# Attention phases beside a token mixer: one inversion step a phase later, one pairing changed, nine products in the last outputs

## The chip, the cores and the metric

The kernel runs on one core of one Trainium2 chip. Its time is the device time of one execution in microseconds, given as the median of several runs. The engines are named as in the profile: PE is TensorE (matmuls; its weight loads are listed apart as PEld), DVE is VectorE, ACT is ScalarE, POOL is GpSimd and SP is SyncE, which here mainly issues DMAs. Each engine works through its own queue of instructions in order and waits at a semaphore when something it needs is not ready.

## The reference

With x of 2048 tokens by 512 channels, the result is a gated sum of two branches, `g * a + (1 - g) * b`.

```
g = sigmoid((x * gate_w).sum(-1))
a: qkv = x @ wqkv, 32 heads of 16 channels
   p = softmax(q k^T * 16**-0.5);  a = concat_heads(p v) @ wo
b: h = layernorm(x);  u = gelu(h^T @ w1 + b1)      (512 x 1792, over tokens)
   b = (u @ w2 + b2)^T                             (2048 x 512)
```

Everything is float32. The kernel keeps that precision in its large products by splitting a number into a high and a low part and adding three products (high by high, high by low, low by high).

## The kernel before, in words

The kernel first projects v, k and q, normalises the rows and runs the first layer of the mixer. This takes the first 300 us or so. The rest, from about 305 us to the end, is the attention, with the second mixer layer and the output projection packed between its instructions. The order of all instructions of this part is written out by hand, so each engine's queue is exactly the order in which the Python loop issues them.

**Groups and phases.** A group is one half of the queries (1024) with one pair of heads; there are 32 groups (16 pairs of heads for each half). A group has 4 phases, so there are 128 phases, numbered 0 to 127 (`LAST`). A phase makes 16 score tiles of 128 keys by 512 queries (n = 0 to 15). A score product uses only 64 of TensorE's 128 rows: head 0 of the pair lies in rows 0 to 63, head 1 in rows 64 to 127. Two products on different halves of the rows can run side by side.

**Dense products beside scores.** Because of that, the first `n_b` scores of a phase are all of one head (head 0 in an even phase, head 1 in an odd one), and beside each of them runs one half of a dense product (`dn`), 64 of its 128 rows. The even phase does one half of the rows, the next odd phase the other half. The remaining 16 − n_b scores alternate between the heads, so that two of them run side by side. The dense products are the second mixer layer up to phase 91 (n_b = 14), none in phases 92 to 95, the output projection of the first 8 row tiles in phases 96 to 111 (n_b = 12, all of a tile's products), and that of the last 8 row tiles in phases 112 to 127. Of those last tiles only a part is done there: 6 products (phases 112 to 117, three tiles) or 8 (phases 118 to 127, five tiles) of the 12. The remaining products, which need the last heads, are done in the tail after phase 127 (`others`, with `early[t]` the number already done). There the last pair of heads is multiplied directly (`last_pair`), and the rows are finished on VectorE and stored (`finish`, line 1039).

**From scores to v.** The 16 score tiles lie in seven PSUM banks, used in turn. Four (n = 1, 3, 5, 7) are copied out by VectorE (line 930) and go through one closing exponential on ScalarE at the end of the phase (line 945, tile `pe`). Six (n = 0, 2, 4, 6, 8, 9) take one ScalarE exponential each (line 934). The last six are taken in three pairs of neighbouring banks, (10, 11), (12, 13) and (14, 15), with one exponential for each pair (line 875), or two in a group's first phase for the first of them (line 878). A bank is free again only when the copy or the exponential that reads it is done; the scores n >= 10 wait for that.

Then `apply_v` multiplies the exponentials with v, pair of tiles by pair of tiles, in the order `TURNS` = (0, 2), (4, 6), (8, 9), (10, 11), (12, 13), (14, 15). The pairs (1, 3) and (5, 7) and the last one are held over to the next phase. In the first phase of a group the held pairs of the previous group are applied first (its final add), then the new group's pairs go to another bank. The product v accumulates in one bank, whose columns are split by head, and VectorE adds the bank to the group's sum `ot` (line 821): one instruction over 512 columns if both heads and both query blocks are met, otherwise one instruction for each part that was met (128 or 64 partitions by 256 columns).

**Sums, inversion and fetching.** v has a column of ones, so the softmax denominators come out as rows of `ot`. When a group is final, `store` writes its outputs and its row sums `r` to DRAM. For every four pairs of heads (one k of 4, for each half of the queries) `invert(half, k, pairs, at)` then brings the sums back (DMA `inv<-r`, line 623, issued in phase p0), clamps and inverts them on VectorE (lines 626 and 627, in the phase `at`, after that phase's copies and before its `ot` add), and stores them again (DMA `ri<-inv`, line 631, in phase `at + 1`). `fetch_o` loads the unnormalised outputs (line 641) and the inverted sums broadcast over 16 rows each (line 642), and lets VectorE multiply, round to the high part and subtract to the low part (line 955). For the second half and k = 2 this is p0 = 113 and `at` = 113; the fetch is called in phase p2 = 114, with its VectorE steps in phases 115, 115 and 116, and `load_wq` in p2 + 4 = 118.

`calls[p]` are issued at the start of phase p, mostly DMAs on SP and a memset on POOL; `later[p]` are VectorE steps issued after the copies of phase p. The lines that decide this:

```
        calls.setdefault(at + 1, []).insert(0, (put_back,))
    ...
            for what, *args in calls.get(p, ()):
    ...
            for what, *args in later.get(p, ()):
    ...
            turns, now_held = ([tuple(units[n] for n in pair) for pair in pairs] for pairs in (order, HELD))
```

Of the kernel before, what the change touches and what calls it, by code (L numbers as in the profile page):

```python
# [59 lines left out]
def gated_mix(ctx: ExitStack, tc: tile.TileContext, a_x, a_wqkv, a_wo, b_w1, b_b1, b_w2, b_b2, gate_w, out):  # L60
# [54 lines left out]
    order = {f0: [(c + (NS // 2 if f0 + NB >= F else 0)) % NS for c in range(NS)] for f0 in range(0, F, NB)}  # L115
# [51 lines left out]
    with tc.tile_pool(name="vp", bufs=1, side="right") as pool:  # L167
# [140 lines left out]
        y, t, w = (pool.tile([P, NS], F32, name=n) for n in "ytw")  # L308
# [34 lines left out]
    with tc.tile_pool(name="ln0", bufs=3, side="right") as ln:  # L343

        def project(w, n):
            ps = bank()
            cols = slice(n * NB, (n + 1) * NB)
            hi, lo = w
            products(ps, [((hi[:, k, :], lo[:, k, :]), (xt_hi[:, k, cols], xt_lo[:, k, cols])) for k in range(ND)])
            return ps  # L350
# [68 lines left out]
    with tc.tile_pool(name="ln1", bufs=3, side="right") as ln, tc.tile_pool(name="gl", bufs=2, side="right") as gl:  # L419
# [29 lines left out]
        for f0, cs in order.items():  # L449
            n = min(NB, F - f0) // P  # L450
# [37 lines left out]
    NP = H // 2  # L488
# [42 lines left out]
    PHASES, NSC, BANKS = 4, 16, 7  # L531
# [15 lines left out]
    def second_layer(t):  # L547

        box = []

        def step(fc, k):
            if fc == 0 and k == 0:
                box.append(ps_dn.tile([P, D], F32, name="dn"))
            if fc % 4 == 0 and k == 0:
                load_weight()
                box.append(ready.pop(0))
            at = slice(fc % 4 * P, (fc % 4 + 1) * P)
            hi, lo = (w[:, at] for w in box[-1])
            a, b = ((hi, u_hi), (hi, u_lo), (lo, u_hi))[k]
            last = fc == NF - 1 and k == 2  # L560
            return box[0], a, b[:, fc, :], fc == 0 and k == 0, last, (lambda: second_out(t, box[0])) if last else None

        return [(step, fc, k) for fc in range(NF) for k in range(3)]
# [4 lines left out]
    def call(at, *what):  # L568
        calls.setdefault(at, []).append(what)
# [140 lines left out]
    def put(steps, at, sizes):  # L710
        for n in sizes:
            dense[at] = [steps.pop(0) for _ in range(n)]
            at += 1
        assert not steps
        return at

    def put_output(t, m, at):
        steps, load = project(t, m)
        call(2 * at - 2, load)
        return put(steps, at, [m])  # L720
# [4 lines left out]
    first, at = steps[:28], put(steps[28:], 0, [14])  # L725
    for t in range(1, NS):
        at = put(second_layer(t), at, [14] * 3)
    for half in range(2):
        for k in range(ND):
            pairs = 3 if half and k == ND - 1 else 4  # L730
            p0 = PHASES * (half * NP + 4 * k + pairs) + 1
            call(p0, invert, half, k, pairs, p0 + (0 if half and k > 1 else 2))
    p0 = 2 * at
    call(p0, open_end)
    on_dve(p0 + 9, end_constants)
# [5 lines left out]
    for t in range(NH):  # L741
        at = put_output(t, 3 * ND, at)
    p1 = PHASES * (NP + 2 * 4) + 3
    call(p1, fetch_o, 1, 0, (8, 9), (p1 + 2, p1 + 3, p1 + 3))
    call(p1 + 4, fetch_o, 1, 1, (10, 11), (p1 + 6, p1 + 7, p1 + 7))
    p2 = PHASES * (NP + 3 * 4) + 2
    assert p2 > 2 * at
    call(p2, fetch_o, 1, 2, (0, 1), (p2 + 1, p2 + 1, p2 + 2))
    call(p2 + 4, load_wq, p2 + 4)
    call(LAST - 1, fetch_o, 1, 3, (2, 3), (LAST, LAST, LAST), 3)  # L750
    for t in range(NH, NS):
        at = put_output(t, 6 if 2 * at < p2 + 3 else 8, at)
    assert at == NG * PHASES // 2

    token = out_pool.tile([1, 1], F32, name="token", bufs=1)
# [4 lines left out]
    TURNS = [(0, 2), (4, 6), (8, 9), *TWO]  # L760
    HELD = [(1, 3), (5, 7)]
# [64 lines left out]
    with tc.manual_schedule(engines=engines):  # L826
# [4 lines left out]
        for n, (step, *args) in enumerate(first):  # L831
            if n and n % 12 == 0:
                split_weight(nc.vector.tensor_copy, nc.vector.tensor_tensor)
            ps, a, b, start, stop, done = step(*args)
# [4 lines left out]
        for p in range(LAST + 1):  # L839
            grp, ph = divmod(p, PHASES)  # L840
            second = ph % 2
            if ph == 0:
                sums[grp] = ot_pool.tile([P, NB], F32, name="ot")
                nc.gpsimd.memset(sums[grp], 0.0)
                at = [[0, 0], [0, 0]]
# [8 lines left out]
            n_b = len(beside)  # L854
            half = slice(0, HALF) if second else slice(HALF, P)

            head = [second if n < n_b else (n - n_b) % 2 for n in range(NSC)]
            qbs = {}
            for a, b in TURNS + HELD:
                if head[a] == head[b]:  # L860
                    qbs[a], qbs[b] = 0, 1
                else:
                    zero, one = (a, b) if head[a] == 0 else (b, a)
                    qbs[zero], qbs[one] = turn, 1 - turn
                    turn = 1 - turn

            swap = ph == PHASES - 1 and p < LAST and n_b == NSC - 2
            order = [*TURNS[:4], TURNS[5], TURNS[4]] if swap else TURNS

            def exps(n):  # L870
                pt = ptp.tile([P, 2, NB], F32, name="p2", bufs=len(TWO) + 1)
# [16 lines left out]
            for n in range(NSC):  # L888
# [31 lines left out]
                if n < n_b:  # L920
                    ps, a, b, begin, last, done = beside[n]
# [218 lines left out]
```

## Time and profile before

| what | value |
|---|---|
| median of 3 runs | 1293.45 us (1293.15 to 1293.7) |
| profiled execution | 1294.68 us |
| its span, first to last instruction | 1292.5 us |
| mean granted TensorE clock | 0.996 |
| busy: PE, ACT, DVE, POOL | 99%, 84%, 52%, 15% of the span |
| HBM traffic | 101 GB/s over the span |

A timeline row gives the start and the time in microseconds, the engine, the line of the kernel, the operation, the tiles written and read, the shapes and the count of merged instructions; in square brackets stands how long the engine had been idle before it and what ended that. SPq and ACTq are DMAs issued by those engines. Times are counted from the start of the span. A wait for several semaphores is put down to the one that came last. Matmul ends are modelled, so the distance between two starts says more than a matmul's own time.

### The profile page before, as it was taken

Reading aid. Unit: us, or ns where it says so; the run is one execution under the profiler, and the core shown is the slowest. Engines: PE = TensorE matmul, PEld = TensorE weight load, DVE = VectorE, ACT = ScalarE, POOL = GpSimd, SP = SyncE. Lnnn points to the kernel's source line nnn. Section 1 sums busy time; section 2 is a strip of 40 time slices with the busy share of each in tenths; the row PEclk is TensorE's granted clock in tenths of the full one; section 3 lists DMA queues with packets and bytes.
Section 4 is the critical chain, followed back from the end, with each engine's and each line's share of the span. In section 5 each row is a group of like instructions: output and inputs, shape, how many; then the busy total and the mean of one; then the engine's idle time right before and its main releaser. Section 6 shows DMA issues by size and latency. Waiting matters only on the chain.

```text
span 1292.5 us, 33044 instructions
## 1 busy us (share of the span) xinstructions
PE 1275.1 (99%) x13276; PEld 838.4 (65%) x13276; DVE 671.4 (52%) x1142; ACT 1088.5 (84%) x1537; POOL 198.0 (15%) x306
## 2 busy tenths in 40 slices
PE   9999999999999999999999999999999999999997
PEld 7888888886666666666666666666665556655555
DVE  5675362437445545445445444544544675545555
ACT  3443343448999999999999999999999999998993
POOL 0210244454111111111111111111110000000000
PEclk9999999999999999999999999999999999998999
DMA  4497643327343343333444433333423755433412
GB/s 131 139 317 277 223 120 98 98 78 160 67 88 76 73 96 83 79 62 82 84 69 89 82 75 60 80 81 68 86 55 87 163 125 121 89 78 88 80 37 79
DMA packets 93581, 133.19 MB, mean 103 GB/s; under 512 B 16277, under 2 KB 55339, under 8 KB 90348
## 3 DMA queue, kind: packets, MB, share of 16 engines
q1 hardware_dynamic: 92844, 129.94, 41.4%
q8 instruction: 107, 1.75, 0.6%
q10 hardware_dynamic: 576, 1.05, 0.2%
q14 instruction: 54, 0.44, 0.1%
HBM read 97.00 MB, written 33.93 MB: 101 GB/s over the span
## 4 chain that ended last, share of the span: by engine, by line
PE 88%; ACT 9%; issue 1%; DVE 1%; SPq 0%; DMA 0%; ACTq 0%
PE av L799 27%; PE s L913 20%; PE acc L417 12%; PE t L913 11%; PE acc L74 10%; PE s L799 4%; ACT p L934 3%; ACT p L875 3%; ACT pe L945 2%; PE dn L922 2%; PE pa L996 1%; PE acc L188 1%; PE dn L835 1%; PE acc L255 0%; DMA inv<-r 0%
## 5 line engine op out<-in xcount | busy, mean ns | idle before, releaser
L934 ACT ACTIVATE p<-s 128x512 f32<-128x512 f32 x768 | 413.2, 783 | 8.1 <-PE s L913 7.8
L875 ACT ACTIVATE p<-t 128x1024 f32<-128x1024 f32 x352 | 365.6, 1264 | 0.0
L913 PE MATMUL s<-qs,ks 64*128 64x512 f32 x1344 | 339.1, 403 | 4.2 <-DVE ot L821 3.6
L930 DVE COPY pe<-s 128x512 f32<-128x512 f32 x512 | 317.8, 682 | 5.6 <-PE s L913 4.9
L913 PEld LDWEIGHTS s<-qs,ks 64*128 64x128 f32 x1344 | 231.9, 184 | 104.1 <-issue 51.9
L799 PE MATMUL av<-p,v 128*32 128x256 f32 x4904 | 289.5, 380 | 0.0
L821 DVE TENSOR_TENSOR ot<-av,ot 128x512 f32<-128x512 f32 (+2 forms) x137 | 83.3, 609 | 393.0 <-PE av L799 392.8
L945 ACT ACTIVATE pe<-pe 128x2048 f32<-128x2048 f32 x129 | 276.8, 2148 | 0.0
L799 PEld LDWEIGHTS av<-p,v 128*32 128x32 f32 x4904 | 159.8, 110 | 106.6 <-issue 2.0
L913 PE MATMUL t<-qs,ks 64*128 64x512 f32 x704 | 180.2, 451 | 4.5 <-DVE pe L930 0.3
L922 PE MATMUL dn<-u_hi,w_lo 64*128 64x512 f32 x430 | 174.8, 406 | 0.0
L922 PE MATMUL dn<-u_lo,w_hi 64*128 64x512 f32 x430 | 174.7, 406 | 0.0
L922 PE MATMUL dn<-u_hi,w_hi 64*128 64x512 f32 x428 | 173.5, 405 | 0.0
L67 POOL TENSOR_TENSOR w_lo<-w_raw,w_hi 128x512 fp32r<-128x512 f32 (+1 forms) x126 | 149.0, 1189 | 124.5 <-ACT w_hi L66 108.0
L913 PEld LDWEIGHTS t<-qs,ks 64*128 64x128 f32 x704 | 89.5, 185 | 91.5 <-ACT p L934 89.9
L926 POOL MEMSET token<- 1x1 f32 x124 | 11.2, 91 | 830.9 <-PE dn L922 739.9
L799 PE MATMUL av<-pe,v 128*32 128x256 f32 x2048 | 138.1, 387 | 0.0
L66 ACT CAST w_hi<-w_raw 128x512 fp32r<-128x512 f32 (+1 forms) x67 | 38.1, 569 | 79.2 <-PE acc L417 58.8
L799 PEld LDWEIGHTS av<-pe,v 128*32 128x32 f32 x2048 | 53.6, 109 | 55.2 <-ACT p L934 31.3
L417 PE MATMUL acc<-h_hi,w_hi 128*128 128x512 f32 x224 | 87.1, 389 | 0.0
L417 PE MATMUL acc<-h_lo,w_hi 128*128 128x512 f32 x224 | 87.1, 389 | 0.0
L417 PE MATMUL acc<-h_hi,w_lo 128*128 128x512 f32 x224 | 87.1, 389 | 0.0
(150 smaller groups left out, 1513.3 us busy)
## 6 DMA issues: line engine op xcount, KB each, us to landing
w_raw<-in_B_w_dram SPq DMA_DIRECT2D x96, 256.0 KB
ks<-kp SPq DMA_DIRECT2D x192, 128.0 KB
qs<-qp SPq DMA_DIRECT2D x256, 64.0 KB
qp<-pc SPq DMA_DIRECT2D x16, 768.0 KB
x<-in_A_x_dram SPq DMA_DIRECT2D x32, 256.0 KB
kp<-pc SPq DMA_DIRECT2D x16, 512.0 KB
w_raw<-in_B_w_dram SPq DMA_DIRECT2D x32, 128.0 KB
bp<-row SPq DMA_DIRECT2D x16, 256.0 KB
```

What stands on the lines that cost most here:

```text
L66: copy(hi, src)
L67: return sub(lo, src, hi.bitcast(F32), ALU.subtract)
L74: nc.tensor.matmul(ps, a, b, start=start and n == 0, stop=stop and n == last)
L417: nc.tensor.matmul(p, a, b, start=first and k == 0, stop=last and k == 2)
L799: mm = nc.tensor.matmul(av[32 * j : 32 * (j + 1), i * QC : (i + 1) * QC], v_flat[:, v_at : v_at + 32], pt[:, h * QC : (h + 1) * QC], start ...
L821: nc.vector.tensor_tensor(x, y, x, ALU.add)
L875: nc.scalar.activation(pt, twos[low, low + 1], AF.Exp, scale=SCALE)
L913: nc.tensor.matmul(s, kt[grp][rows_i, c * P : (c + 1) * P], qt[grp][rows_i, qb * NB : (qb + 1) * NB], start=True, stop=True,)
L922: mm = nc.tensor.matmul(ps, a[half], b[half], start=begin and not second, stop=last and bool(second))
L930: nc.vector.tensor_copy(pt, s)
L934: nc.scalar.activation(pt, s, AF.Exp, scale=SCALE)
L945: nc.scalar.activation(x, x, AF.Exp, scale=SCALE)
```

## The change

There are three edits. The first gives the inversions of the second half their VectorE phases from a table: k = 2 moves from `p0` to `p0 + 1`, the others stay. p2, from which the third fetch and `load_wq` are counted, moves from 114 to 115, and everything counted from it moves along. The second edit replaces, in the first phase of a group with 12 dense products, the last two pairs (12, 13), (14, 15) by (12, 14), (13, 15); with 12 dense products n = 12 and 14 are head 0, and 13 and 15 are head 1. The exponentials are still taken over neighbouring banks. The third edit gives the last five output tiles 9 instead of 8 of their 12 products in phases 118 to 127. Since 9 is odd, the scores that alternate between heads start with the other head in odd phases, so that both heads come to the same count over a group; for an even n_b that formula gives what it gave before. The `swap` case (a group's last phase, n_b = 14) is written differently and gives the same order as before.

```diff
-            call(p0, invert, half, k, pairs, p0 + (0 if half and k > 1 else 2))
+            call(p0, invert, half, k, pairs, p0 + (2, 2, 1, 0)[k] if half else p0 + 2)
...
-    p2 = PHASES * (NP + 3 * 4) + 2
-    assert p2 > 2 * at
+    p2 = PHASES * (NP + 3 * 4) + 3
+    assert p2 >= 2 * at - 1
     call(p2, fetch_o, 1, 2, (0, 1), (p2 + 1, p2 + 1, p2 + 2))
     call(p2 + 4, load_wq, p2 + 4)
...
-        at = put_output(t, 6 if 2 * at < p2 + 3 else 8, at)
+        at = put_output(t, 6 if 2 * at < p2 + 3 else 9, at)
...
-            head = [second if n < n_b else (n - n_b) % 2 for n in range(NSC)]
+            head = [second if n < n_b else (n - n_b + second * n_b) % 2 for n in range(NSC)]
             qbs = {}
-            for a, b in TURNS + HELD:
+            order = list(TURNS)
+            if ph == 0 and n_b == NSC - 4:
+                order[-2:] = (12, 14), (13, 15)
+            for a, b in order + HELD:
...
             swap = ph == PHASES - 1 and p < LAST and n_b == NSC - 2
-            order = [*TURNS[:4], TURNS[5], TURNS[4]] if swap else TURNS
+            if swap:
+                order[-2:] = order[:-3:-1]
```

## The prediction

> **What bounds the kernel now.** I read the page first (engine shares, then the chain that ended last), then stretches of the attention part, the starts of one ScalarE instruction that comes once a phase, and finally the instruction timelines where that beat is broken.
>
> ```profile
> PE 1275.1 (99%) x13276; PEld 838.4 (65%) x13276; DVE 671.4 (52%) x1142; ACT 1088.5 (84%) x1537; POOL 198.0 (15%) x306
> PE 88%; ACT 9%; issue 1%; DVE 1%; SPq 0%; DMA 0%; ACTq 0%
> ```
>
> TensorE is busy nearly always by its records and holds the chain, but that share is an average over stages and a busy TensorE need not be the limit. The view by stretches gives four phases of the stage with 14 dense products a phase, four of the stage with 8, a short stretch that turns out to matter, and one in which to look for DMA traffic. Its columns are busy time of PE, weight loads, DVE, ACT and POOL, then granted clock, DMA share and GB/s.
>
> ```profile
> 957.20:987.10 29.90, 29.90 (x380) 18.46 (x378) 13.30 (x23) 29.90 (x42) 2.82 (x7) 1.00 0.27 50
> 1196.90:1226.80 29.90, 29.12 (x356) 17.06 (x354) 16.60 (x27) 29.90 (x43) 0.89 (x5) 1.00 0.41 75
> ...
> 1165.70:1172.50 6.80, 6.63 (x52) 3.12 (x54) 1.39 (x3) 5.87 (x7) 0.00 (x0) 0.50 0.63 171
> ...
> 1174.20:1177.70 3.50, 3.24 (x26) 1.84 (x23) 3.50 (x7) 3.40 (x7) 0.62 (x2) 1.00 0.00 0
> ```
>
> ScalarE is busy without a hole in both normal stretches (29.90 of 29.90). Its exponentials set the beat of a phase, whether TensorE has 14 dense products to run or 8. So an edit to a phase is worth nothing unless it makes ScalarE wait or stops it from waiting. The place where it waits shows in the closing exponential of a phase (line 945), here of phases 111, 113 and 115:
>
> ```profile
> 1143.20 2.00 ACT L945 ACTIVATE pe<-pe 128x2048 f32<-128x2048 f32 x1
> 1158.20 2.03 ACT L945 ACTIVATE pe<-pe 128x2048 f32<-128x2048 f32 x1
> 1179.95 1.98 ACT L945 ACTIVATE pe<-pe 128x2048 f32<-128x2048 f32 x1
> ```
>
> Two phases take 15.00 us from 1143.20 to 1158.20, and 21.75 from 1158.20 to 1179.95: 6.75 us are lost in phases 114 and 115. The timeline there, merged from its engines:
>
> ```profile
> 1157.40 0.37 SPq L623 DMA_DIRECT2D inv<-r  x1
> ...
> 1155.25 0.74 DVE L676 SCALAR_TENSOR_TENSOR base<-dn,g,base 128x512 f32<-128x512 f32 x1
> 1163.38 0.20 DVE L626 TENSOR_SCALAR inv<-inv 128x64 f32<-128x64 f32 x1 [7.38 <-DMA inv<-r]
> 1163.61 0.55 DVE L627 RECIPROCAL inv<-inv 128x64 f32<-128x64 f32 x1
> 1164.08 0.63 DVE L821 TENSOR_TENSOR ot<-av,ot 128x512 f32<-128x512 f32 x1
> ...
> 1164.76 0.18 PEld L913 LDWEIGHTS s<-qs,ks 64*128 64x128 f32 x2 [4.01 <-DVE ot L821]
> 1165.35 1.70 ACT L934 ACTIVATE p<-s 128x512 f32<-128x512 f32 x3 [3.65 <-PE s L913]
> ...
> 1164.19 0.34 SPq L631 DMA_DIRECT2D ri<-inv  x1
> 1166.23 0.63 SPq L642 DMA_DIRECT2D o_sum<-ri  x1
> ```
>
> VectorE stands at the head of its queue in phase 113, waiting for a small transfer (the row sums, `inv`) that is issued at 1157.40 and lands at 1163.38. Behind it, in order, stands the add of phase 113 (line 821) and the copies of phase 114; they free the PSUM banks that TensorE's scores need (4.01 us idle), and ScalarE waits for the scores (3.65 us). Then the granted clock is 0.50 for 6.8 us, and phase 115 comes late too. ScalarE's wait explains about 3.7 of the 6.75; the other 3.1 follow in the half-clock stretch.
>
> **The change part by part.**
>
> *The third inversion a phase later.* The load of the sums stays where it is (call of phase 113). The clamp and reciprocal on VectorE go to phase 114, their store to phase 115, the two loads of `fetch_o` on SP to 115 (behind the base-row load of phase 114 instead of ahead of it), and VectorE's multiply, rounding and subtraction to 116, 116 and 117.
> VectorE's rows of phases 115 and 116 as they are now:
>
> ```profile
> 1177.67 1.21 DVE L955 TENSOR_TENSOR o_sum<-e,o_sum 128x1024 f32<-128x1024 f32 x1
> 1178.91 0.69 DVE L955 CAST e<-o_sum 128x1024 fp32r<-128x1024 f32 x1
> 1181.40 0.69 DVE L821 TENSOR_TENSOR ot<-av,ot 128x512 f32<-128x512 f32 x1 [1.79 <-PE av L799]
> 1182.10 2.48 DVE L930 COPY pe<-s 128x512 f32<-128x512 f32 x4
> 1186.72 0.88 DVE L821 TENSOR_TENSOR ot<-av,ot 128x256 f32<-128x256 f32 x2 [1.01 <-PE av L799]
> ```
>
> In phase 114 VectorE will finish its copies one beat (7.5 us) after it finished those of 113; row 1155.25 ends at 1155.99 and phase 114 has no output to write (its tile ends in the odd phase), so it arrives about 0.7 us sooner, near 1162.7, and waits until 1163.38. The 0.75 us of work end near 1164.2. What is queued behind, the add of phase 114, needs that phase's last products. In phase 115 the add starts 1.45 after the closing exponential (1181.40 against 1179.95); for 114 that is 1158.20 + 7.5 + 1.45 = 1167.15. Cover: 3 us. The stall goes whole, and with it the TensorE idle time ahead of the half clock: **−6.75 us**. Bounds: at worst the 3.65 alone (if the clock fell for another reason), at best 6.75.
> Late next: the store of the reciprocals still leaves when VectorE is done, at 1164.2 as now, and the broadcast load at 1166.2. No DMA moves between 1174.20 and 1177.70, so both fetched tiles are in by 1174.2. VectorE will want them after the copies of phase 116: 1182.10 less the 6.75 saved, plus 2.4 of copies, is 1177.75. It then has 1.9 us of work (1.21 and 0.69) ahead of the add of the held units, which comes 4.6 us after the copies start (1186.72 against 1182.10), where 2.4 + 1.9 = 4.3 fit. Cost nothing, upper bound 0.3.
>
> `load_wq` follows by a phase (118 to 119): one POOL memset behind one more token write, four SP loads behind the base-row load of 118, the split on VectorE from 120 to 121. The split was in a group's first phase, which has the early add; 121 has none, and its consumer is the tail. Nothing.
>
> A rule to weigh here: the Trainium skill, "TensorE: Matmul & The Clock Gate", section "What's actually happening", says that one idle window of about 3.4 us halves the TensorE clock and one busy window of that length gives it back. The trace agrees on the trigger (4.01 us idle, then 0.50) but shows 6.8 us at half clock, twice what that page gives. By that page only half of the 3.1 us would belong to the clock, the stall would be worth an estimated 5.2 and the forecast would be 1286.6; the measured beats decide, and I keep 6.75.
>
> *Pairing by heads.* In the first phase of the four groups with 12 dense products (phases 96, 100, 104, 108) the fifth pair applied is now (12, 14), both head 0, where (12, 13) had a head each. VectorE's add after it then covers one column half, one instruction instead of two. The pair needs exponential (14, 15) instead of (12, 13).
>
> ```profile
> 1058.34 2.03 ACT L875 ACTIVATE p<-t 128x1024 f32<-128x1024 f32 x2
> 1059.14 2.34 PE L799 MATMUL s<-p,v 128*32 128x256 f32 x40
> 1061.60 0.86 DVE L821 TENSOR_TENSOR ot<-s,ot 128x256 f32<-128x256 f32 x2 [1.33 <-issue]
> 1062.50 2.48 DVE L930 COPY pe<-s 128x512 f32<-128x512 f32 x4
> ...
> 971.46 0.42 DVE L821 TENSOR_TENSOR ot<-s,ot 128x256 f32<-128x256 f32 x1 [1.79 <-PE s L799]
> 972.10 2.48 DVE L930 COPY pe<-s 128x512 f32<-128x512 f32 x4 [0.21 <-PE s L913]
> ```
>
> With 14 dense products it is already one add, 0.42 us, and the copies wait for a score, not for the add; with 12 the adds run 0.86 and the copies start at their end. The saving is 0.44 us of VectorE time right ahead of the copies. What that costs the beat now, by the closing exponential of phases 100 and 112:
>
> ```profile
> 1060.15 2.01 ACT L945 ACTIVATE pe<-pe 128x2048 f32<-128x2048 f32 x1
> 1150.75 2.00 ACT L945 ACTIVATE pe<-pe 128x2048 f32<-128x2048 f32 x1
> ```
>
> Three groups take 90.60 us, 30.20 each, against 30.00 for four phases at the 15.00 of two found above: 0.20 each. I take **−0.6** for the three; bounds 0 (something else makes them long) and 0.9 (all four groups, rounded up). On the other side, exponential (14, 15) ends at 1058.34 + 2.03 = 1060.37, and the fifth of five pairs starts at 1059.14 + 4/5 × 2.2, about 1060.9: 0.5 us of cover, no wait. If the cover went, up to one pair (0.45) in each of four phases: +1.8.
>
> *Nine products.* Five output tiles take 9 instead of 8 products each into the phases 118 to 127, half of one in each phase: a row-half matmul of about 0.23 us.
>
> ```profile
> PEld t L913 <- ACT p L934: 1.1, 3, 0.4
> PEld av L799 <- ACT p L934: 0.2, 1, 0.2
> ...
> 1197.49 0.39 PE L913 MATMUL s<-qs,ks 64*128 64x512 f32 x1
> 1197.72 0.39 PE L913 MATMUL s<-qs,ks 64*128 64x512 f32 x1
> ```
>
> The slot is 1197.72 − 1197.49 = 0.23. The score order becomes nine beside products, one alone, then pairs: 13 slots for 12. In phase 118 TensorE waits 1.3 us for ScalarE (the two rows from the view of waits), so the slot is hidden; the stretch with 14 products, 15 slots, kept the same beat. Cost 0, upper bound 10 × 0.23 = 2.3. The alternation turned round in the odd phases only balances the two heads.
> In return the tail has five matmuls fewer:
>
> ```profile
> 1277.82 0.36 DVE L1009 TENSOR_TENSOR e<-o_sum,e 128x256 fp32r<-128x256 f32 x1
> 1278.29 1.68 PE L1026 MATMUL pa<-e,e 16*128 16x512 f32 x24
> 1284.32 0.75 DVE L1039 SCALAR_TENSOR_TENSOR base<-pa,g,base 128x512 f32<-128x512 f32 x1 [0.38 <-PE pa L996]
> 1286.18 0.75 DVE L1039 SCALAR_TENSOR_TENSOR base<-pa,g,base 128x512 f32<-128x512 f32 x1 [0.18 <-PE pa L996]
> ```
>
> Two (tiles 4 and 6) lie ahead of the first last-pair products, which start at 1278.29. Starting 0.46 earlier is possible: the low part they need, done at 1278.18, is used only by the last 8 of the 24, 1.1 us in. Three (tiles 3, 5, 7) lie at the end, where the outputs follow TensorE 0.93 apart ((1286.18 − 1284.32)/2). With three matmuls a tile TensorE needs 0.70, and VectorE's 0.75 takes over: 0.23 + 2 × 0.18 = 0.59. Together **−1.05**; bounds 0.46 (closer output transfers eat the rest) and 5 × 0.23 = 1.15.
>
> Sum: −6.75 − 0.6 − 1.05 = −8.4. The profiled execution took 1294.68 (span 1292.5), so 1286.3; the median of the runs shown, 1293.45, is 1.23 below it, so **1285.1**.
>
> **The rivals.**
> *(a) The ninth product is not hidden:* the odd count splits a pair, the single score stands alone, and the slot reaches ScalarE. 1285.1 + 2.3 = 1287.4. Against it: the 1.3 us of waits.
> *(b) The new pair waits for its exponential:* gain 0.6 lost, 1.8 added, 1287.5. The 0.5 us of cover speak against it.
> *(c) The wait for the sums shrinks but stays,* or VectorE waits in phase 116 for the broadcast: with half of 6.75 left, 1288.5. A margin row for such waits is the fourth inversion, which this change leaves:
>
> ```profile
> 1255.60 0.19 DVE L626 TENSOR_SCALAR inv<-inv 96x64 f32<-96x64 f32 x1 [3.02 <-DMA inv<-r]
> ```
>
> There the transfer lands 3 us after VectorE asks, and the beat holds; any delay of that phase's stores adds directly, a few tenths at most.
> *(d) The change does not do what it says:* the load slips with the phases and lands as late against them; only the other two parts count, 1293.45 − 1.65 = 1291.8.
> *(e) Slower:* one mechanism, the broadcast of the reciprocals landing so late that VectorE blocks in phase 116 ahead of the early add. It decides when the loss passes 8.4 us: a stall of 5.3 plus the half clock's 3.1, that is landing after about 1177.7 + 0.3 + 5.3 = 1183.3, 9 us after traffic ends in this trace. Landing 2 us later still gives 1295.5.
>
> **How the numbers follow.** Forecast 0.76, with a range of its own of 1284.3 to 1286.2 (terms at their bounds of 0.9 and 1.15 below, 0.3 and 0.6 plus some tenths from the fourth inversion above). (a) 0.07, (b) 0.06, (c) 0.06, (d) 0.02, (e) 0.03. Range 1284.0 to 1287.6: it takes in the forecast, (a) and (b), with run scatter of 0.3 below. About 0.2%, 2.6 us, can be told from no change. Faster: 0.76 + 0.07 + 0.06 + 0.06 = 0.95; within: (d) 0.02; slower: (e) 0.03.
>
> **What would show it.** Closing exponentials 7.5 apart through phases 113 to 117, no 4 us idle of weight loads, granted clock 1.00 up to the end; a short wait of about 0.7 us for `inv` in phase 114. One 0.42 us add in phases 97, 101, 105, 109, copies within 0.1 of the previous phase's closing exponential, groups of 30.0. Phases 118 to 127 at 7.5 with TensorE's waits shortened by 0.2. Last outputs 0.75 apart. It would be wrong if a half-clock stretch remains, if VectorE waits for the broadcast in 116, or if phases 118 to 127 lengthen to 7.7.

## The result, and the profile after

The changed kernel takes 1287.07 us (median of 5 runs, 1286.48 to 1287.85), against 1293.7 us (1293.15 to 1294.52, 5 runs) for the kernel before, measured beside it. The ratio is 0.9949, with a 95% interval of 0.9934 to 0.9963: it is faster by 6.6 us, or 0.5%. The forecast was 1285.1, with a range of 1284.0 to 1287.6. The sign and the mechanism were right and the time lies in the range, 2 us above the forecast; it lies above the narrower range of the forecast itself, which ended at 1286.2. Profiled execution against profiled execution, it went from 1294.68 to 1287.07.

In the changed kernel all lines behind the edits lie four further on: the closing exponential is line 949, the scores 917, the copies 934, the single exponentials 938, the tail's last-pair products 1030 and finishing instructions 1043. The closing exponentials of phases 111, 113 and 115, from the timeline of ScalarE (start, time, line, tile, shapes):

```profile
1142.54 2.19 ACT L949 ACTIVATE pe<-pe 128x2048 f32<-128x2048 f32 x1
1157.52 2.23 ACT L949 ACTIVATE pe<-pe 128x2048 f32<-128x2048 f32 x1
1172.51 2.20 ACT L949 ACTIVATE pe<-pe 128x2048 f32<-128x2048 f32 x1
```

Two phases now take 14.98 and 14.99 us; the 21.75 are gone. The stretch of phases 114 to 116 (busy PE, weight loads, DVE, ACT, POOL, then clock, DMA share, GB/s):

```profile
1157.50:1180.00 22.50, 22.29 (x266) 13.11 (x262) 13.42 (x22) 22.50 (x32) 0.80 (x4) 1.00 0.48 110
```

ScalarE is busy for all of its 22.50 us, and the granted clock is 1.00. VectorE in phases 113 to 116:

```profile
1154.57 0.74 DVE L676 SCALAR_TENSOR_TENSOR base<-dn,g,base 128x512 f32<-128x512 f32 x1
1158.99 0.69 DVE L821 TENSOR_TENSOR ot<-av,ot 128x512 f32<-128x512 f32 x1 [3.68 <-PE av L799]
1159.69 2.48 DVE L934 COPY pe<-s 128x512 f32<-128x512 f32 x4
1162.39 0.20 DVE L626 TENSOR_SCALAR inv<-inv 128x64 f32<-128x64 f32 x1 [0.21 <-DMA inv<-r]
1162.62 0.55 DVE L627 RECIPROCAL inv<-inv 128x64 f32<-128x64 f32 x1
1166.49 0.69 DVE L821 TENSOR_TENSOR ot<-av,ot 128x512 f32<-128x512 f32 x1 [3.31 <-PE av L799]
...
1177.08 1.22 DVE L959 TENSOR_TENSOR o_sum<-e,o_sum 128x1024 f32<-128x1024 f32 x1
1178.32 0.69 DVE L959 CAST e<-o_sum 128x1024 fp32r<-128x1024 f32 x1
1179.31 0.89 DVE L821 TENSOR_TENSOR ot<-av,ot 128x256 f32<-128x256 f32 x2 [0.29 <-PE av L799]
```

The wait for the sums is 0.21 us, and 3.31 us of VectorE's time are free before the next add. Phase 116 does not wait for the broadcast; its early add still finds VectorE idle (0.29), so the two steps of 1.9 us just fit. In phase 101 one add has gone:

```profile
1061.58 0.42 DVE L821 TENSOR_TENSOR ot<-s,ot 128x256 f32<-128x256 f32 x1 [1.33 <-issue]
1062.22 1.89 DVE L934 COPY pe<-s 128x512 f32<-128x512 f32 x3 [0.21 <-PE s L917]
```

By the ends of the closing exponentials, no phase from 1 to 126 is longer than 7.55 us. Before, phases 102, 106 and 110 took 7.68 to 7.70, phase 114 took 11.37 and phase 115 10.34. From the end of phase 0 to the end of phase 126 it is 944.40 us instead of 951.79: 7.39 less, where 6.75 + 0.6 had been forecast. The last part of the tail:

```profile
1270.55 1.67 PE L1030 MATMUL pa<-e,e 16*128 16x512 f32 x24
...
1275.45 0.75 DVE L1043 SCALAR_TENSOR_TENSOR base<-pa,g,base 128x512 f32<-128x512 f32 x1 [1.13 <-PE pa L1030]
1276.35 2.12 DVE L1043 SCALAR_TENSOR_TENSOR base<-pa,g,base 128x512 f32<-128x512 f32 x3 [0.15 <-PE pa L1000]
```

The last three finishing instructions run without a gap, 0.7 us apart. The first last-pair products start 7.74 us earlier than before (1278.29 there); counted from the end of phase 126 that is 0.5 earlier, as forecast (0.46). VectorE's last finishing instruction ends 21.3 us after the end of phase 126; before it was 22.5. So far 8.6 us are saved (7.39 + 1.24), a little more than forecast. But the span is only 7.6 shorter: from the last finish to the end of the span it now takes 6.4 us, and before 5.6 (the rest is 0.2 at the start). That loss, and the smaller difference of the medians (6.6), were what the experiments had to explain.

### The profile page after: what moved, and what is told of

It is laid out like the page before. It is cut to its first block, busy times and chain, and to the rows that moved or that the text cites. A ratio compares the mean times of both kernels' runs of the same rounds, so it can differ in the third digit from the quotient of the medians.

```text
span 1284.9 us, 33049 instructions
## 1 busy us (share of the span) xinstructions
PE 1272.5 (99%) x13281; PEld 837.1 (65%) x13281; DVE 670.8 (52%) x1138; ACT 1087.6 (85%) x1537; POOL 199.1 (15%) x306
## 3 DMA queue, kind: packets, MB, share of 16 engines
q10 hardware_dynamic: 576, 1.05, 0.2%
## 4 chain that ended last, share of the span: by engine, by line
PE 94%; ACT 4%; issue 1%; DVE 0%; DMA 0%; SPq 0%; ACTq 0%
PE av L799 29%; PE s L917 23%; PE t L917 12%; PE acc L417 12%; PE acc L74 10%; PE s L799 5%; PE dn L926 2%; ACT p L879 1%; ACT p L938 1%; ACT pe L949 1%; PE pa L1000 1%; PE dn L835 1%; PE acc L188 1%; PE acc L255 0%; PE pa L1030 0%
## 5 line engine op out<-in xcount | busy, mean ns | idle before, releaser
L879 ACT ACTIVATE p<-t 128x1024 f32<-128x1024 f32 x352 | 370.5, 1300 | 0.0
L917 PEld LDWEIGHTS s<-qs,ks 64*128 64x128 f32 x1344 | 234.7, 184 | 99.7 <-issue 52.2
L949 ACT ACTIVATE pe<-pe 128x2048 f32<-128x2048 f32 x129 | 280.9, 2181 | 0.0
```

Source lines behind the costliest of these rows:

```text
L879: nc.scalar.activation(pt, twos[low, low + 1], AF.Exp, scale=SCALE)
L917: nc.tensor.matmul(s, kt[grp][rows_i, c * P : (c + 1) * P], qt[grp][rows_i, qb * NB : (qb + 1) * NB], start=True, stop=True,)
L949: nc.scalar.activation(x, x, AF.Exp, scale=SCALE)
```

## The experiments

The theory at the outset was the prediction's sum: 6.75 for the stall, 0.6 for the pairs, 1.05 for the nine products. The rivals were that the stall is usually smaller than in the one execution it was read from, that the tail's saving is lost after the last finish, and, for the half clock, that phase 115 had been late for another reason. Medians stand beside those of the kernel before on the same chip.

**The first edit alone.**

```diff
-            call(p0, invert, half, k, pairs, p0 + (0 if half and k > 1 else 2))
+            call(p0, invert, half, k, pairs, p0 + (2, 2, 1, 0)[k] if half else p0 + 2)
...
-    p2 = PHASES * (NP + 3 * 4) + 2
+    p2 = PHASES * (NP + 3 * 4) + 3
```

> The first edit alone: the third inversion of the second half on VectorE a phase later, with the fetch and the weights of the last pair behind it. Theory: the whole stall goes, phases 114 and 115 take 7.5 us each, no half clock between 1160 and 1180, the closing exponential of phase 126 ends 6.75 us earlier than in the profile of before, and the median falls by 5.5 to 6.8. Rival (the edit's gain is smaller than the stall because something else takes its place): the beat shows 7.5 in 114 and 115 but other phases lengthen, median down by less than 4.5.

Measured: 1288.68 us against 1294.56, ratio 0.9954 (0.994 to 0.9967), 5.9 us less. Phases 114 and 115 are at the beat, and only 102, 106 and 110 still take 7.70. From phase 0 to 126 it is 945.14 us, 6.65 less than in the profile of before. The theory holds and nothing takes the stall's place.

**The second edit alone.**

```diff
-            for a, b in TURNS + HELD:
+            order = list(TURNS)
+            if ph == 0 and n_b == NSC - 4:
+                order[-2:] = (12, 14), (13, 15)
+            for a, b in order + HELD:
...
-            order = [*TURNS[:4], TURNS[5], TURNS[4]] if swap else TURNS
+            if swap:
+                order[-2:] = order[:-3:-1]
```

> The second edit alone: pairs (12, 14) and (13, 15) in four first phases. Theory: phases 102, 106 and 110 take 7.48 us instead of 7.7, the adds ahead of the copies in phases 97, 101, 105 and 109 are one of 0.42 us, the beat gains 0.6, and the median about as much, at the edge of what can be told. Rival (the pair waits for exponential 14, 15): TensorE waits in phases 96, 100, 104, 108, gain 0 or a loss of up to 1.

Measured: 1293.16 against 1294.56, ratio 0.999 (0.9981 to 0.9999). The phases 102, 106 and 110 are at 7.48, and no other phase up to 126 but 114 and 115 is over 7.6 (phase 127 takes 7.81 in this trace, which puts its last finish 0.3 later in the table further down). The add ahead of the copies in phase 101, from VectorE's timeline of this kernel:

```profile
1062.02 0.42 DVE L821 TENSOR_TENSOR ot<-s,ot 128x256 f32<-128x256 f32 x1 [1.33 <-issue]
1062.66 1.89 DVE L934 COPY pe<-s 128x512 f32<-128x512 f32 x3 [0.22 <-PE s L917]
```

The beat gains 0.65 (three times 7.70 − 7.48). The median's 1.4 has an interval from 0.1 to 2.5, so the trace is the better measure. The profiled execution is shorter by more than that, but for another reason: phases 114 and 115, which this edit does not touch, lost 5.45 us in it and not 6.75.

**The third edit alone.**

```diff
-        at = put_output(t, 6 if 2 * at < p2 + 3 else 8, at)
+        at = put_output(t, 6 if 2 * at < p2 + 3 else 9, at)
...
-            head = [second if n < n_b else (n - n_b) % 2 for n in range(NSC)]
+            head = [second if n < n_b else (n - n_b + second * n_b) % 2 for n in range(NSC)]
```

> The third edit alone: nine products in the five last outputs. Theory: phases 118 to 127 keep 7.48 to 7.54 us, the last finishing VectorE instruction comes 1.05 to 1.25 us earlier after the closing exponential of phase 126, and the median falls by at most that. Rival (what the tail saves is lost after the last finish, in stores and in what comes after them): the last VectorE finish is 1.1 earlier and the median moves by less than 0.4.

Measured: 1293.81 against 1294.56, ratio 0.9993 (0.9984 to 1.0003). Phases 118 to 127 keep the beat, and the last finish comes 21.32 after phase 126 (1.2 gained), but the end comes 6.3 after that. By the trace it keeps some 0.5 of the 1.2 us; the median's 0.75 has an interval that includes no gain at all. Its profile also shows a shorter half clock after the stall than the profile of before:

```profile
1158.00:1167.20 9.20, 5.24 (x66) 2.83 (x57) 2.84 (x6) 5.50 (x8) 0.09 (x1) 1.00 0.60 75
1167.30:1170.70 3.40, 3.33 (x26) 1.50 (x28) 0.74 (x2) 3.40 (x6) 0.00 (x0) 0.51 0.63 200
1170.80:1178.00 7.20, 6.93 (x90) 3.87 (x84) 4.47 (x7) 5.81 (x9) 0.62 (x2) 1.00 0.23 63
```

**The kernel before again.** No edit.

> The kernel before, unchanged, for a second trace. If the profiled execution was a long one of its kind (it stands 1.0 to 1.2 us above the median), this trace shows where it was long: theory, in the time from the last VectorE finish to the end of the span, or in the start-up before 300 us, with the stall again 6.75. Rival: the stall itself varies, and is 5.5 to 6 here.

Measured: 1294.34 against 1294.56. Theory and rival both miss the number, 6.28, but the rival is right in kind: the stall itself varies. With the span of 1292.6 this execution is as long as the first, though phases 114 and 115 lose 0.47 less in it. The loss by the ends of the closing exponentials (two normal phases: 14.96), in every trace that has VectorE's long wait in phase 113:

```
                       phase 114  phase 115   loss   half clock
before                   11.37      10.34     6.75     6.83 us
before again             11.49       9.75     6.28     6.83 us
pairs only               11.10       9.31     5.45     6.83 us
nine only                11.39       9.02     5.45     3.41 us
before, gap filled       11.30       7.80     4.14     none
```

Phase 114 loses the same everywhere, 3.6 to 4.0; what varies is phase 115, 1.5 to 2.9 where the clock fell. The half clock begins between 1163.6 and 1167.3 in these traces, earlier or later within the stall and the work after it, and lasts 3.41 us or twice that. TensorE's weight loads pause for 3.65 to 4.10 us in the four traces where the clock fell, and it fell 3.0 to 5.7 us after the last of them. The times of further executions fit with a stall that differs from run to run: of the 27 executions of the kernel before on this chip, the 15 with a mean granted clock of 0.995 or 0.996 have a median of 1295.0 us, and the 12 with 0.997 or 0.998 one of 1294.3; that mean also counts the clock after the last work, so it is a hint only.

**The gap filled.** The last row of that table.

```diff
+            if p == PHASES * (NP + 3 * 4) + 2:
+                fill = ps_dn.tile([P, D], F32, name="dn")
+                for _ in range(16):
+                    nc.tensor.matmul(fill, wo_hi[:, 0, :P], wo_hi[:, 0, :], start=True, stop=True)
             if not second:
```

> The kernel before with 16 matmuls whose result is read by nothing, put on TensorE ahead of the scores of phase 114, about 3.7 us of work where it otherwise stands idle 4 us. VectorE's wait stays. Theory (of the 5.4 to 6.75 us that phases 114 and 115 lose, only the wait of some 3.9 is the stall, and the rest is the half clock that follows from the idle time): no stretch at clock 0.50 near 1165, phase 115 back to 7.5, the two phases lose 3.7 to 4.3 together, the median 1.5 to 2.8 lower than before. Rival (phase 115 is late for want of data or banks, and the clock only goes with it): the loss of phase 115 stays at 1.5 or more.

Measured: 1292.71 against 1294.81, ratio 0.9986 (0.9976 to 0.9995), 2.1 us less. VectorE's wait is still there, the clock stays at 1.00, and phase 115 comes back to 7.80:

```profile
1158.00:1165.00 7.00, 7.00 (x66) 5.06 (x56) 1.36 (x4) 3.28 (x4) 0.00 (x0) 1.00 0.57 63
1165.00:1172.00 7.00, 6.62 (x83) 3.59 (x81) 2.70 (x5) 6.93 (x9) 0.09 (x1) 1.00 0.64 171
```

```profile
1163.58 0.20 DVE L626 TENSOR_SCALAR inv<-inv 128x64 f32<-128x64 f32 x1 [7.19 <-DMA inv<-r]
```

So 16 matmuls that compute nothing make the kernel faster. Most of the second part of the stall is the clock's, and TensorE's idle time sets it off; the rival, that data or banks made phase 115 late, falls. The 0.3 us that phase 115 still loses stand at full clock and are not explained. The trigger agrees with the Trainium skill ("TensorE: Matmul & The Clock Gate", section "What's actually happening"), which halves the clock after at least one idle window of about 3.4 us. The length of the gap alone does not say when the clock falls, though: in the trace with the pairs only, the clock is 0.50 from 1163.57 on, 3.0 us after the last weight load ended and before the next one starts at 1164.18.

**The load ahead of the next group's k.** Phase 113's `invert` call is issued before `load_k`; nothing else moves.

```diff
+            ahead = p == PHASES * (NP + 3 * 4) + 1
+            if ahead:
+                for what, *args in calls.get(p, ()):
+                    what(*args)
             if ph == 1 and grp + 1 < NG:
                 kt[grp + 1] = load_k(grp + 1)
-            for what, *args in calls.get(p, ()):
-                what(*args)
+            if not ahead:
+                for what, *args in calls.get(p, ()):
+                    what(*args)
```

> The kernel before with one order changed on SP: in phase 113 the load of the row sums is issued ahead of the six loads of the next group's k, not behind them. VectorE's clamp and reciprocal stay in phase 113. Theory (the load was late because 768 KB stood before it in the same queue): it lands about 3 us after its issue, as the fourth inversion's does, VectorE still waits but not long enough to hold its add, phases 114 and 115 take 7.5 to 7.8, the median falls by 5 to 6.5 as with the first edit alone. Rival (the load is late because the stores of the sums are): it lands as late as before, near 1163, and nothing is gained.

Measured: 1289.65 against 1294.81, ratio 0.9963 (0.9949 to 0.9977), 5.2 us less. From the timelines of SP and VectorE:

```profile
1155.92 0.33 SPq L623 DMA_DIRECT2D inv<-r  x1
1156.29 2.76 SPq L508 DMA_DIRECT2D ks<-kp  x6
...
1157.76 0.20 DVE L626 TENSOR_SCALAR inv<-inv 128x64 f32<-128x64 f32 x1 [1.58 <-DMA inv<-r]
1157.99 0.55 DVE L627 RECIPROCAL inv<-inv 128x64 f32<-128x64 f32 x1
1159.82 0.69 DVE L821 TENSOR_TENSOR ot<-av,ot 128x512 f32<-128x512 f32 x1 [1.28 <-PE av L799]
```

The load lands 1.8 us after its issue instead of 6.0. The six loads ahead of it, 768 KB, had made it late, not the stores of the sums. VectorE stays in phase 113 and its wait is harmless. Phase 115 takes 7.80 in this trace, at full clock. The order alone doesn't make it so: the last kernel below has the same order on SP, and its phase 115 takes 7.49. Why it is 7.80 here stays open.

**Short last stores.** In the changed kernel, tiles 3, 5 and 7 store 128 of 512 columns.

```diff
-            queue.dma_start(dst, row)
+            n = P if t in LATE else D
+            queue.dma_start(dst[:, :n], row[:, :n])
```

> The changed kernel with the last three stores (tiles 3, 5, 7) cut to 128 of 512 columns; the other columns of these rows are not written. With nine products the time from VectorE's last finish to the end of the span was 6.2 to 6.3 us against 5.1 to 5.6 without, and the code that follows the closing branch came 4.1 us after it against 3.1 to 3.5. Theory (the code's fetch waits behind the last stores' packets, which now come closer together): with a quarter of these bytes the fetch starts within 1.2 us of the last finish, not 1.7, the branch takes 3.5 or less, the end comes 5.6 or less after the last finish. Rival (the place of the code decides, not the stores): fetch, branch and end as in the changed kernel, 6.2.

Measured: 1286.02, against 1287.25 for the changed kernel on the same chip. VectorE's last instructions are as close as there, so only the stores differ:

```profile
1277.08 2.12 DVE L1043 SCALAR_TENSOR_TENSOR base<-pa,g,base 128x512 f32<-128x512 f32 x3 [0.15 <-PE pa L1000]
```

The closing branch and the first instruction behind it on VectorE, from the view of the branch's line in this kernel and in the changed one (first and last start behind the durations):

```profile
L1068 DVEq COMPARE_BRANCH  x1: 76/76/76, 1279.1 to 1279.1; - x1
L1068 DVEq EVENT_SEMAPHORE  x1: 21/21/21, 1282.4 to 1282.4; - x1
```

```profile
L1067 DVEq COMPARE_BRANCH  x1: 76/76/76, 1278.6 to 1278.6; - x1
L1067 DVEq EVENT_SEMAPHORE  x1: 21/21/21, 1282.7 to 1282.7; - x1
```

It is 3.3 us in the one and 4.1 in the other. In the kernel before, with eight products, it is 3.5:

```profile
L1063 DVEq COMPARE_BRANCH  x1: 76/76/76, 1286.8 to 1286.8; - x1
L1063 DVEq EVENT_SEMAPHORE  x1: 21/21/21, 1290.3 to 1290.3; - x1
```

By the DMA packets, the first of the 8 KB blocks on an instruction queue, taken here for the code behind the branch, starts 0.92 us after the last finish with short stores, and 1.74 and 1.82 in the changed kernel's two traces. VectorE's load of the flag that the branch tests, just ahead of it, takes 0.54 us with short stores and 0.81 and 0.83 with full ones. The end comes 5.7 after the last finish, 0.1 above what was expected, and 6.2 to 6.4 in the changed kernel's two traces.

**The changed kernel again.** No edit.

> The changed kernel again, beside the three others: a second trace of its end. Theory: no phase over 7.6, the last finish 21.4 after the closing exponential of phase 126, the end 6.2 to 6.4 after that, and the median 7 to 8 below before's of the same chip, as the three edits alone added up to 8.

Measured: 1287.25 against 1294.81, ratio 0.9945 (0.9928 to 0.9961), 7.6 us less. No phase is over 7.6, the last finish comes 21.33 after phase 126 and the end 6.2 after that.

**Without nine products, and nine for two tiles.** The first two edits with `8`; and the changed kernel with the line below. The loop's even tiles from 12 on are the tail's tiles 4 and 6.

```diff
-        at = put_output(t, 6 if 2 * at < p2 + 3 else 9, at)
+        at = put_output(t, 6 if 2 * at < p2 + 3 else 9 if t % 2 == 0 else 8, at)
```

> The first two edits without the third: eight products in the last five outputs. Theory: no phase over 7.6, the last finish 22.5 after the closing exponential of phase 126 (21.4 with nine), the end 5.1 to 5.6 after that (6.0 to 6.3 with nine), so 0.3 to 0.7 slower than the changed kernel: the third edit's 1.1 us keeps only about half. Rival (nine is hidden nowhere and buys nothing): equal to the changed kernel or faster.

> The changed kernel with nine products only for the two tiles whose work lies ahead of the first last-pair products (tiles 4 and 6 of the tail), eight for tiles 3, 5 and 7. Theory: the last finish 22.0 to 22.1 after the closing exponential of phase 126 (0.46 gained), and since the last outputs are again 0.93 apart, the end 5.1 to 5.6 after it; in all as fast as the changed kernel within 0.4. Rival (the end is late for another reason than the spacing of the last stores, such as where the code lies): the end 6.0 or more after the last finish.

Measured, on one chip: 1288.24 without (ratio to before 0.9948, 0.9934 to 0.9961) and 1287.70 with nine for two tiles (0.9944, 0.9931 to 0.9958). Last finish (the end of the last finishing instruction; the 21.4 of the expectations is the end of the flag load, up to 0.1 us later) and end:

```
                        last finish      from there      from phase 126
                        after phase 126  to the end      to the end
eight: before                22.5           5.6              28.1
eight: before again          22.5           5.3              27.8
eight: inversion only        22.5           5.6              28.1
eight: pairs only            22.8           5.2              27.9
eight: gap filled            22.5           5.4              27.9
eight: load ahead            22.5           5.9              28.4
eight: without nine          22.5           5.9              28.4
nine for two tiles           22.0           5.5              27.6
nine: changed kernel         21.3           6.4              27.7
nine: again                  21.3           6.2              27.5
nine: nine only              21.3           6.3              27.6
nine, short stores           21.3           5.7              27.0
```

With nine products in five tiles the last finish is 1.2 us earlier, and the end follows 6.3 us after it on average, against 5.6 with eight. About 0.5 is left. With nine for only two tiles the last outputs keep their distance and the end costs 5.5: in its one trace it keeps all its 0.5, and lies where the full edit does. The end with eight was expected at 5.1 to 5.6 and came at 5.9 twice, so it scatters by some 0.7 of its own. From phase 126 to the end, the traces with nine (27.5 to 27.7) and with eight (27.8 to 28.4) do not overlap. The medians can't tell the third edit: without it the ratio to before is 0.9948, and for the changed kernel it is 0.9949 and 0.9945 on other chips, so the 0.3 to 0.7 that was expected is not seen there.

**The load ahead, and eight products a tile earlier.** The second and third edit with the load ahead in place of the first edit; the third fetch then stays a phase earlier. The line below is the one that is new, against the kernel before.

```diff
-        at = put_output(t, 6 if 2 * at < p2 + 3 else 8, at)
+        at = put_output(t, 9 if 2 * at >= p2 + 3 else 8 if 2 * at > p2 else 6, at)
```

> The second and third edit with the load of the sums issued ahead of the next group's k in place of the first edit; the third fetch then comes a phase earlier, and the output tile of phases 116 and 117 takes 8 products instead of 6. Theory: two matmuls less ahead of the first last-pair products, 0.46 us, against some 0.3 that phase 115 lost with this order before; the last finish 20.9 to 21.0 after the closing exponential of phase 126, the median within 0.5 of the changed kernel's, more likely below. Rival: the fetch comes too late for phase 116, phases 116 or 117 lengthen by 0.5 or more, and it is slower than the changed kernel.

Measured: 1286.67 (1286.38 to 1287.22), ratio to before 0.9938 (0.9924 to 0.9951). No phase up to 126 is over 7.6, the last finish comes 20.95 after phase 126, as expected, and the end 6.2 after that. On its chip it is 1.6 us below the kernel without nine products and 1.0 below nine for two tiles. It has the lowest median of the kernels with the whole computation here. The changed kernel wasn't run on that chip, and the two ratios to before overlap, so that it beats the changed kernel is likely but not shown.

## Why the prediction was right, and where it was off

*The stall* (−6.75). Right in its mechanism: the wait at the head of VectorE's queue, the idle TensorE, the half clock, the cover of 3 us in phase 114 (3.31 seen), the wait of 0.7 left there (0.21 seen, the load landed 5.6 us after its issue instead of 6.0), the broadcast in time for phase 116. Off in size. The term was read from one execution, and that execution has the largest loss of the four unfilled traces, 5.45 to 6.75. The first edit alone is worth 5.9 by medians. The sum was then moved by 1.23 to the median, as if the profiled execution were merely slower everywhere. As far as its excess lay in the stall, it is gone with the stall and should not have been subtracted: 1294.68 − 8.4 = 1286.3 is 0.8 below the 1287.07 measured. The traces allow this only in part, since the kernel before again has as long a span with 0.47 less of stall. As measured, the three terms are 5.9, 0.65 and about 0.5, some 7.1 in all where 8.4 had been forecast; the medians show 6.6 and, on another chip, 7.6.

*The range.* The time lies inside 1284.0 to 1287.6, but 0.9 above the 1286.2 at which the forecast's own range ended. The upper end came from rivals (a) and (b), at 1287.4 and 1287.5, and neither of them happened, so that it caught the result is in part luck. The forecast's own range left out the lower bound of 3.65 that the prediction itself gave for the stall and that leads to 1288.2. Its lower end is a slip too: the terms named for it give 1284.7, not 1284.3.

*How much of the stall is the clock's.* The prediction held the measured 6.8 us against the Trainium skill's window of about 3.4 us and kept 6.75. The runs show one window and two windows, 3.41 and 6.83 us. The skill's shorter figure gave 5.2 for the stall, and two traces have 5.45; the truth lies between, and changes from run to run. The forecast worked out from it, 1286.6, came closer to 1287.07 than the 1285.1 that was kept. The page asks for at least one busy window, so two do not go against it. The clock records of all thirteen traces show one thing more: the time between two changes of the clock is always a whole multiple of 3.413 us (in the kernel before 340 of them, then 2 at half clock, then 34). How these steps lie against the stall differs between executions, which would fit one step or two after the same stall. No run sets that place, so it is not shown.

*The pairs* (−0.6): 0.65 in the beat. The new pair does not wait for its exponential; rival (b) is out.

*Nine products* (−1.05). The cost was rightly put at nothing: the beat of phases 118 to 127 holds, and rival (a) is out. TensorE's longest group of waits in phase 118, which was 1.1 us in the prediction's row, is now shorter by the forecast 0.2:

```profile
PEld t L917 <- ACT p L938: 0.9, 3, 0.3
```

The gain in TensorE's and VectorE's work was right too, 1.2 us at the last finish. What failed is the step from the last finish to the end, which the sum took as fixed; the lower bound of 0.46 for closer output transfers was the right place and the right size. Some 0.7 us are lost there. In all four traces with nine products in five tiles and full stores, the flag load takes 0.81 to 0.83 us and the first code block starts 1.7 to 1.8 us after the last finish; in all others it is 0.54 to 0.55, and 0.9 to 1.1 (1.4 once). That both are early again with a quarter of the bytes in the last three stores speaks for a queue of store packets before them. It rests on one kernel with short stores, and the scatter of the end is as large as the effect. It can't be the whole account either: with the load ahead and eight products, the code block starts at 1.1 and the branch still takes 4.0 us. So it is likely rather than settled.

Rivals (c), (d) and (e) are out: the remaining wait is 0.21 us, the load does not slip with the phases, and VectorE doesn't wait for the broadcast.

## What to carry to other kernels

A small load that an in-order engine waits for should be issued ahead of the bulk loads of its queue, or be asked for later; here either was worth over 5 us, and what is late is seen in the issue and landing of that one transfer. Where a stall idles TensorE as long as here, 3.65 to 4.10 us between weight loads, count the half clock after it separately and as a range, from several traces, since it differed from one execution to the next. A range that is put together from rivals should also hold the worst bound of each term of the sum. A saving at the very end is worth what the time from the last instruction to the end of the span leaves of it.

## What the runs showed that was not expected

Sixteen matmuls without use, put into an idle stretch of 4 us, made the kernel 2.1 us faster, by keeping the clock at 1.00. The half clock came in lengths of 3.41 and 6.83 us for stalls of the same 3.6 to 4.0 us, and began at different places of it, once only 3.0 us after TensorE's last weight load. On VectorE, the first instruction behind the closing branch came 3.1 to 4.4 us after the branch, several times the last output's 0.75 us of VectorE work. No run leaves the branch out, so what it costs the kernel is not shown.
